# Reordering the opening of a fused retention and MoE kernel: constants, masks, one load and the weight triggers

## The chip, the cores and the metric

The kernel runs on one core of a Trainium2 chip. The metric is the device time of one execution in microseconds. The kernel before the change was run six times: the median is 203.0 us, the lowest 202.28 us, the highest 203.25 us.

A core has five engines that run their own instruction streams in order: TensorE (PE: matrix products and transposes, with weight loads as a row of their own, PEld), VectorE (DVE), ScalarE (ACT), GpSimd (POOL) and SyncE (SP, here only a queue that issues DMAs). They wait for each other by semaphores. ScalarE, GpSimd and SyncE issue DMAs too; each issuing instruction stands in its engine's stream, and whatever follows it there waits for the issue (not for the landing).

## What is computed

```python
# attention: B=4, H=8, S=768, D=64; gamma_h = 1 - 2**(-5-h)
for t in range(S):
    state = gamma * state + outer(k[:, :, t], v[:, :, t])     # D x D per batch and head
    y[:, :, t] = 1/sqrt(D) * q[:, :, t] @ state
x = y.transpose(0, 2, 1, 3).reshape(B * S, H * D)             # 3072 x 512
h = x @ w_in                                                  # 512 -> 2048
g = 0.5 * h * (1 + tanh(sqrt(2/pi) * (h + 0.044715 * h**3)))
out = g @ w_out                                               # 2048 -> 512, 3072 x 512 f32
```

## The kernel before, in words

The sequence of 768 tokens is cut into six chunks of C = 128 tokens. For a chunk c and a batch b the attention is done in matrix form: q and k are scaled by powers of gamma and rounded to fp16 (`prep1`, lines 146 to 164), transposed by TensorE (`mm_T`, line 187) and copied out of PSUM (`ev_T`), multiplied to a 128 x 128 matrix A per head (`mm_A`, line 207), masked with a decay triangle (`ev_A`, line 220, which reads `mask`), and multiplied with v (`mm_yi`, line 242). `ev_Y` writes the result, transposed, to `xT[c]`: that is the input of the first MoE product. `mm_s` and `ev_S` carry the state to the next chunk.

The first MoE product of a chunk has 16 column blocks of w_in; `moe1_two(c, fp, t0, t1)` does blocks 2fp and 2fp+1 for the tokens of two batches (8 matmuls of 128x256, line 349) and one Gelu on ScalarE (line 369). `moe1_four` does four blocks for one batch. w_in comes in four tiles of four blocks each: `w_in0` serves fp 0 and 1, `w_in1` fp 2 and 3, `w_in2` fp 4 and 5, `w_in3` fp 6 and 7. The second product uses sums of g (`g_sums`, line 399) and of w_out (`w_sums`), a product scheme with seven block products in place of eight (`units_0` for chunk 0, `units_w` for the others).

The order on every engine is the order of the calls in the source (`manual_schedule`). This case is about the opening, chunk 0, in these places:

- Lines 96 to 104: loads at the start. On SyncE's queue: k of batch 0, the identity `iden`, k of batch 1, v of batch 1, k of batch 2. On ScalarE's queue: q of batch 0, the constants `cst` (74 KB: the row scales for q and k, the triangle), q of batch 1, v of batch 0; and from line 723 q of batch 2.
- `spin(n)` (line 113): n matmuls of zeros with zeros into a PSUM bank that nobody reads. They keep TensorE busy.
- `masks()` (line 126): eight instructions on VectorE, each scales the triangle in `cst` by a constant of one head. `ev_A` of batch 0 needs all eight.
- `prep1(VE, "q", 0, b)` (VectorE) and `prep1(PO, "k", 0, b)` (GpSimd): the scaled q and k of chunk 0. Both read `cst`.
- `load_w_in(i)` and `load_w_out(i)` (lines 328 and 336): 512 KB each as it lands in fp16, issued by GpSimd between its `prep1` calls. GpSimd also loads v of batch 2 and all of batch 3.
- Lines 740 to 796: the attention of chunk 0, batch by batch, with `spin` calls between, then the first MoE product of chunk 0 with the attention of batches 2 and 3 laid between its parts. `t01` is the tokens of batches 0 and 1, `t2` those of batch 2, `t3` those of batch 3.

After the opening, lines 798 to 1042 run the remaining second and first products and the attention of the later chunks; the change doesn't touch them.

Of the kernel before, what the change touches and what calls it, by code (L numbers as in the profile page):

```python
# [16 lines left out]
def kernel(  # L17
# [9 lines left out]
    nc = tc.nc  # L27
# [21 lines left out]
    cst_h = nc.inline_tensor(cst_np, name="rr_cst")  # L49
# [16 lines left out]
    OQ, OK, OG, OT = 0, H, 2 * H, 2 * H + NHP  # L66


    misc = const.tile([128, 32], F32)
    cst = const.tile([128, 192], F32)  # L70
# [8 lines left out]
    def ld_tile(nm, c, b):  # L79
        if (nm, c, b) not in raw:  # L80
            tag, n = ("v1" if nm == "v" else "qk1", 5 if nm == "v" else 8) if c == 1 else (f"{nm}32", 4)
            raw[nm, c, b] = ld.tile([128, H, Dh], F32, tag=tag, bufs=n, name=f"{nm}32")
        return raw[nm, c, b]

    def load1(eng, nm, c, b):
        eng.dma_start(
            out=ld_tile(nm, c, b),
            in_=srcs[nm][b, :, c * C:(c + 1) * C, :].rearrange("h p d -> p h d"),
        )

    def load(c):
        for b in range(B):
            for nm in "qkv":
                load1(nc.sync, nm, c, b)

    load1(nc.sync, "k", 0, 0)
    load1(nc.scalar, "q", 0, 0)
    nc.scalar.dma_start(out=cst[:, :OT + 128], in_=cst_h.ap())
    nc.sync.dma_start(out=iden, in_=iden_h.ap())
    load1(nc.scalar, "q", 0, 1)  # L100
    load1(nc.sync, "k", 0, 1)
    load1(nc.scalar, "v", 0, 0)
    load1(nc.sync, "v", 0, 1)
    load1(nc.sync, "k", 0, 2)


    zero = const.tile([128, 512], F16, name="zero")
# [2 lines left out]
        out=misc[:, 0:1], in_=zero[:, 0:1], func=AF.Gelu_apprx_tanh, scale=1.0  # L110
    )

    def spin(n):
        ps = bank("h", shape=(128, 512), name="spin_ps")
        for _ in range(n):
            nc.tensor.matmul(
                out=ps, lhsT=zero[:, 0:128], rhs=zero, start=True, stop=True
            )
# [7 lines left out]
    def masks():  # L126
        for j in range(2):
            for hp in range(NHP):
                nc.vector.tensor_scalar(  # L129
                    out=mask[:, j, hp],  # L130
                    in0=cst[:, OT:OT + 128],
                    scalar1=float(1.0 / g128[2 * hp + j]),
                    scalar2=None,
                    op0=ALU.mult,
                )

    h16 = {}
    qk16 = {}

    def copy_on(eng, out, in_):  # L140
        if eng is nc.scalar:
            eng.copy(out=out, in_=in_)  # L142
        else:
            eng.tensor_copy(out=out, in_=in_)

    def prep1(eng, nm, c, b):
        if nm == "v":
            t = pre.tile([128, H, Dh], F16, tag="v16", bufs=6, name="v16")
        else:
            if (c, b) not in qk16:  # L150
                qk16[c, b] = pre.tile([128, 2, H, Dh], F16, tag="qk16", bufs=6, name="qk16")
            t = qk16[c, b][:, "qk".index(nm)]
        src = ld_tile(nm, c, b)
        if (nm == "v") == (c < 1):
            copy_on(eng, t, src)
        else:
            col = OQ if nm == "q" else OK
            eng.tensor_tensor(  # L158
                out=t,
                in0=src,  # L160
                in1=cst[:, col:col + H].unsqueeze(2).broadcast_to([128, H, Dh]),
                op=ALU.mult,
            )
        h16[nm, c, b] = t
# [11 lines left out]
    def bank(tag, dt=F32, shape=(128, NHP, 128), name="ps"):  # L176
        return psum.tile(list(shape), dt, tag=tag, bufs=BANKS[tag], name=name)
# [38 lines left out]
    def ev_A(c, b):  # L216
        ps = pss.pop(("A", c, b))
        for j in range(2):
            s = att.tile([128, NHP, 128], F16, tag=f"a{j}", bufs=2, name=f"a_sb{j}")
            nc.vector.tensor_tensor(out=s, in0=ps[j], in1=mask[:, j], op=ALU.mult)  # L220
            a_sb[c, b, j] = s
# [29 lines left out]
    def ev_Y(c, b, eng=nc.vector):  # L251
        if c not in xT:
            xT[c] = xp.tile([128, NHP, B * C], F16, tag="x", bufs=2, name="xT")
        x, ps = xT[c][:, :, b * C:(b + 1) * C], pss.pop(("Y", c, b))
        if c < 1:
            copy_on(eng, x, ps)
        else:
            nc.vector.tensor_tensor(out=x, in0=ps, in1=dec, op=ALU.mult)  # L258
# [15 lines left out]
    def ev_S(c, bs, engs=(nc.vector, nc.vector)):  # L274
        if c + 1 >= NCk:
            return
        s_ps = pss.pop(("S", c, bs))
        for j in range(2):
            sl = slice(j * 64, (j + 1) * 64)
            t = st[sl, bs[0]:bs[-1] + 1, :, j]  # L280
            if c == 0:
                copy_on(engs[j], t, s_ps[sl])
                continue
            for hp in range(NHP):
                nc.vector.scalar_tensor_tensor(  # L285
                    out=t[:, :, hp],
                    in0=t[:, :, hp],
                    scalar=cst[sl, OG + hp:OG + hp + 1],
                    in1=s_ps[sl, :, hp],
                    op0=ALU.mult,  # L290
                    op1=ALU.add,
                )
# [35 lines left out]
    def load_w_in(i):  # L328
        nc.gpsimd.dma_start(
            out=w_in_sb[i],  # L330
            in_=moe_w_in.rearrange("(kc p) n -> p kc n", p=128)[
                :, :, w_in_at[i] * 128:(w_in_at[i] + w_in_n[i]) * 128
            ],
        )
# [11 lines left out]
    def moe1_mm(c, fc, out, t0, t1):  # L346
        wi, wr = w_in_of[fc]
        for kc in range(NHP):
            nc.tensor.matmul(  # L349
                out=out,  # L350
                lhsT=w_in_sb[wi][:, kc, wr * 128:(wr + 1) * 128],
                rhs=xT[c][:, kc, t0:t1],
                start=(kc == 0),
                stop=(kc == NHP - 1),
                skip_group_check=True,
            )

    def g_tile(c, fc):
        r = fc % 8 // 2 * 2
        return g_sb[fc // 8][:, r:r + 2]  # L360

    def g_q(c, r, b, i):
        if (r, b) == (1, 1) and c > 2 and c % 2:
            return g_odd[:, 4 * i:4 * i + 4]
        g = g_sb[i].rearrange("p (f r) (a b t) -> p r b f a t", r=2, a=2, b=2)
        return g[:, r, b]

    def gelu(out, in_):
        nc.scalar.activation(out=out, in_=in_, func=AF.Gelu_apprx_tanh, scale=1.0)  # L369
# [6 lines left out]
    def moe1_two(c, fp, t0, t1):  # L376

        h_ps = bank("h", shape=(128, 2, B * C // 2), name="h_ps")
        for r in range(2):
            moe1_mm(c, 2 * fp + r, h_ps[:, r, 0:t1 - t0], t0, t1)  # L380
        gelu(g_tile(c, 2 * fp)[:, :, t0:t1], h_ps[:, :, 0:t1 - t0])
# [16 lines left out]
    def tt(eng, out, in0, in1, op):  # L398
        eng.tensor_tensor(out=out, in0=in0, in1=in1, op=op)  # L399
# [8 lines left out]
    def g_sums(eng, c, f0, f1, p0=0, p1=2, keys=(1, 2, 3, 4)):  # L408
        i = f0 % 4
        q = {  # L410
            (r, b): g_q(c, r, b, f0 // 4)[:, i:i + f1 - f0, p0:p1]
            for r in range(2)
            for b in range(2)
        }
        t = {j: s_g[j][:, f0:f1, p0:p1] for j in s_g}
        ops = (
            (1, q[0, 1], q[1, 1], ALU.add),
            (2, t[1], q[0, 0], ALU.subtract),
            (3, q[0, 0], q[0, 1], ALU.subtract),
            (4, q[1, 0], t[2], ALU.subtract),  # L420
        )
        for j, in0, in1, o in ops:
            if j in keys:
                tt(eng, t[j], in0, in1, o)
# [284 lines left out]
    def loads(eng, c, *what):  # L709
        for nm, b in what:  # L710
            load1(eng, nm, c, int(b))
# [7 lines left out]
    VE, AC, PO, SY = nc.vector, nc.scalar, nc.gpsimd, nc.sync  # L719
# [1 line left out]


    load1(AC, "q", 0, 2)
    spin(8)
    prep1(VE, "q", 0, 0)
    masks()
    prep1(PO, "k", 0, 0)
    load_w_in(0)
    prep1(PO, "k", 0, 1)
    loads(PO, 0, "v2")  # L730
    load_w_in(1)
    loads(PO, 0, "k3", "q3", "v3")
    load_w_in(2)
    prep1(PO, "k", 0, 2)
    load_w_in(3)
    prep1(PO, "k", 0, 3)
    for i in range(NO):
# [5 lines left out]
    spin(3)  # L743
    mm_A(0, 0)
    ev_A(0, 0)
    spin(2)
    mm_T(0, 1)
    ev_T(0, 1, AC)
    prep1(AC, "v", 0, 0)
    spin(3)  # L750
    mm_A(0, 1)
    ev_A(0, 1)
    mm_yc(0, 0, "o")
# [1 line left out]
    prep1(AC, "v", 0, 1)  # L755
    ev_Y(0, 0, AC)
    prep1(VE, "q", 0, 2)
    spin(3)
    mm_yc(0, 1, "o")
    mm_yi(0, 1)  # L760
    mm_s(0, (0, 1), "o")
    ev_Y(0, 1, AC)

    t01, t2, t3, t23 = (0, half), (half, half + C), (half + C, 2 * half), (half, 2 * half)
    moe1_two(0, 0, *t01)
# [14 lines left out]
    mm_T(0, 3)  # L780
    ev_T(0, 3)
    prep1(AC, "v", 0, 3)
    g_sums(VE, 0, 0, 4, 0, 1, (1, 2))
    moe1_four(0, 1, *t2)
    moe1_two(0, 4, *t01)
    mm_A(0, 3)
    ev_A(0, 3)
    g_sums(VE, 0, 0, 4, 0, 1, (3, 4))
    moe1_two(0, 5, *t01)
    moe1_two(0, 6, *t01)  # L790
    mm_yc(0, 3, "o")
    mm_yi(0, 3)
    mm_s(0, (2, 3))
    ev_Y(0, 3)
    ev_S(0, (2, 3))
    moe1_two(0, 7, *t01)

    nc.gpsimd.tensor_copy(out=dec[0:1, 0, 0:1], in_=w_out_sb[3][0:1, 0, 0:1])
# [274 lines left out]
```

## Time and profile before

| what | value |
|---|---|
| median of six runs | 203.0 us |
| the profiled execution, its own time | 202.28 us |
| its span, first to last instruction | 200.4 us |
| time of that execution outside the span | 1.9 us |
| PE busy | 192.4 us, 96% of the span |
| DVE, ACT, POOL busy | 138.4, 117.7, 137.6 us |
| granted TensorE clock | 1.000 |
| first matmul of the MoE product starts | 15.21 us into the span |

Two things help to read it. The profile page's second part cuts the span into 40 slices of 5 us and gives the busy tenths: PE is at 7 in the first three slices and at 9 in all the others but the last. And the granted clock is 1.00 in every row, yet the zero matmuls of the first 8 us start about 0.43 us apart and those after 11 us about 0.22 us apart, so a half-speed start of TensorE is seen in the durations and not in that column.

### The profile page before, as it was taken

Reading aid. Unit: us, or ns where it says so; the run is one execution under the profiler, and the core shown is the slowest. Engines: PE = TensorE matmul, PEld = TensorE weight load, DVE = VectorE, ACT = ScalarE, POOL = GpSimd, SP = SyncE. Lnnn points to the kernel's source line nnn. Section 1 sums busy time; section 2 is a strip of 40 time slices with the busy share of each in tenths; the row PEclk is TensorE's granted clock in tenths of the full one; section 3 lists DMA queues with packets and bytes.
Section 4 is the critical chain, followed back from the end, with each engine's and each line's share of the span. In section 5 each row is a group of like instructions: output and inputs, shape, how many; then the busy total and the mean of one; then the engine's idle time right before and its main releaser. Section 6 shows DMA issues by size and latency. Waiting matters only on the chain.

```text
span 200.4 us, 5117 instructions
## 1 busy us (share of the span) xinstructions
PE 192.4 (96%) x2067; PEld 153.4 (77%) x2067; DVE 138.4 (69%) x279; ACT 117.7 (59%) x214; POOL 137.6 (69%) x139
## 2 busy tenths in 40 slices
PE   7779999999999999999999999999999999999993
PEld 2347898877888888745478887888888888888883
DVE  0976699969792449997997975995925945227720
ACT  2266654473589409266657698379494496777321
POOL 3995933945189998769947929389979299598200
PEclk9999999999999999999999999999999999999999
DMA  6999999999996699999989989941400130002205
GB/s 153 287 231 273 206 207 263 343 326 211 328 218 137 153 205 257 184 294 249 208 174 228 214 193 226 101 155 66 105 3 0 77 136 0 0 3 106 108 3 206
DMA packets 83255, 34.25 MB, mean 171 GB/s; under 512 B 75936, under 2 KB 80416, under 8 KB 83232
## 3 DMA queue, kind: packets, MB, share of 16 engines
q1 hardware_dynamic: 71696, 18.65, 44.0%
q0 software_dynamic: 6944, 13.63, 25.5%
q10 hardware_dynamic: 4592, 1.65, 3.1%
q8 instruction: 16, 0.26, 0.6%
q14 instruction: 7, 0.06, 0.1%
HBM read 27.63 MB, written 6.29 MB: 169 GB/s over the span
## 4 chain that ended last, share of the span: by engine, by line
PE 89%; DVE 5%; DMA 2%; ACT 2%; issue 1%; ACTq 0%; DVEq 0%
PE o_ps L510 31%; PE h_ps L349 20%; PE h_ps L592 19%; PE y_ps L242 4%; PE a_ps L207 3%; PE o_ps L630 3%; PE o_ps L663 3%; PE y_ps L229 2%; DMA cst<-rr_cst 2%; DVE mask L129 2%; PE qkT_ps L187 2%; DVE a_sb L220 1%; PE s_ps L266 1%; DVE qk L158 1%; DVE xT L258 1%
## 5 line engine op out<-in xcount | busy, mean ns | idle before, releaser
L349 PE MATMUL h_ps<-xT,w_in 128*128 128x256 f16 (+2 forms) x352 | 45.9, 282 | 0.4 <-ACT xT L142 0.4
L369 ACT ACTIVATE g<-h_ps 128x512 f16<-128x512 f32 x52 | 31.0, 600 | 19.7 <-PE h_ps L349 18.0
L399 POOL TENSOR_TENSOR s_g<-g 128x512 f16<-128x512 f16 x30 | 35.3, 1183 | 7.5 <-ACT g L369 6.5
L220 DVE TENSOR_TENSOR a_sb<-a_ps,mask 128x512 f16<-128x512 f32 x48 | 30.5, 683 | 13.3 <-PE a_ps L207 11.9
L349 PEld LDWEIGHTS <-w_in 128*128 128x128 f16 x352 | 30.4, 98 | 10.8 <-issue 0.6
L510 PEld LDWEIGHTS <-s_g 128*128 128x128 f16 x320 | 30.7, 98 | 4.2 <-POOL s_g L399 0.3
L369 ACT ACTIVATE g<-h_sb 128x512 f16<-128x512 f32 x36 | 21.9, 632 | 17.5 <-DVE h_sb L399 17.3
L399 DVE TENSOR_TENSOR h_sb<-h_ps,h_sb 128x512 f32<-128x512 f32 x36 | 22.9, 684 | 9.6 <-ACT h_sb L142 8.9
L510 PE MATMUL o_ps<-t_w,s_g 128*128 128x256 f16 x240 | 29.4, 273 | 0.0
L158 POOL TENSOR_TENSOR v<-v,cst 128x512 f16<-128x512 f32 x20 | 20.5, 1046 | 7.5 <-DMA v<-in_v_dram 3.8
L510 PEld LDWEIGHTS <-g 128*128 128x128 f16 x208 | 20.2, 98 | 2.5
L399 POOL TENSOR_TENSOR s_g<-s_g,g 128x512 f16<-128x512 f16 x18 | 20.9, 1162 | 1.4
L399 POOL TENSOR_TENSOR s_g<-g,s_g 128x512 f16<-128x512 f16 x18 | 20.6, 1154 | 0.0
L592 PEld LDWEIGHTS <-t_in 128*128 128x128 f16 x192 | 18.0, 98 | 2.9
L142 ACT COPY h_sb<-h_ps 128x512 f32<-128x512 f32 x36 | 19.1, 598 | 1.3 <-PE h_ps L592 1.3
L510 PE MATMUL o_ps<-w_out,g 128*128 128x256 f16 x160 | 19.1, 273 | 0.0
L285 DVE SCALAR_TENSOR_TENSOR st<-st,cst,s_ps 64x128 f16<-64x128 f16 x64 | 18.2, 346 | 0.2
L592 PE MATMUL h_ps<-s_x,t_in 128*128 128x256 f16 x144 | 17.8, 273 | 0.0
L258 DVE TENSOR_TENSOR xT<-y_ps,dec 128x512 f16<-128x512 f32 x20 | 13.3, 684 | 5.4 <-PE y_ps L242 5.3
L592 PEld LDWEIGHTS <-w_in 128*128 128x128 f16 x144 | 14.1, 98 | 1.8
L142 ACT CAST qk<-q 128x512 f16<-128x512 f32 x20 | 12.6, 631 | 2.2 <-DMA q<-in_q_dram 2.2
L142 ACT CAST qk<-k 128x512 f16<-128x512 f32 x20 | 12.6, 630 | 0.1
(81 smaller groups left out, 274.8 us busy)
## 6 DMA issues: line engine op xcount, KB each, us to landing
out_dram<-o_sb POOLq DMA_DIRECT2D x10, 512.0 KB, 3.2
k<-in_k_dram SPq DMA_DIRECT2D x19, 256.0 KB, 4.8
v<-in_v_dram SPq DMA_DIRECT2D x17, 256.0 KB, 4.6
q<-in_q_dram SPq DMA_DIRECT2D x16, 256.0 KB, 5.0
w_in<-in_moe_w_in_dram POOLq DMA_DIRECT2D x4, 512.0 KB, 8.3
w_out<-in_moe_w_out_dram POOLq DMA_DIRECT2D x4, 512.0 KB, 10.7
v<-in_v_dram POOLq DMA_DIRECT2D x6, 256.0 KB, 7.0
k<-in_k_dram POOLq DMA_DIRECT2D x5, 256.0 KB, 7.6
```

What stands on the lines that cost most here:

```text
L142: eng.copy(out=out, in_=in_)
L158: eng.tensor_tensor(out=t, in0=src, in1=cst[:, col:col + H].unsqueeze(2).broadcast_to([128, H, Dh]), op=ALU.mult,)
L207: nc.tensor.matmul(out=ps[j][:, hp], lhsT=t[j * 64:(j + 1) * 64, 1, hp], rhs=t[j * 64:(j + 1) * 64, 0, hp], start=True, stop=True,)
L220: nc.vector.tensor_tensor(out=s, in0=ps[j], in1=mask[:, j], op=ALU.mult)
L242: nc.tensor.matmul(out=y_ps[j * 64:(j + 1) * 64, hp], lhsT=h16["v", c, b][:, 2 * hp + j], rhs=a_sb[c, b, j][:, hp], start=(c == 0), stop=True,
L258: nc.vector.tensor_tensor(out=x, in0=ps, in1=dec, op=ALU.mult)
L285: nc.vector.scalar_tensor_tensor(out=t[:, :, hp], in0=t[:, :, hp], scalar=cst[sl, OG + hp:OG + hp + 1], in1=s_ps[sl, :, hp], op0=ALU.mult, ...
L349: nc.tensor.matmul(out=out, lhsT=w_in_sb[wi][:, kc, wr * 128:(wr + 1) * 128], rhs=xT[c][:, kc, t0:t1], start=(kc == 0), stop=(kc == NHP - ...
L369: nc.scalar.activation(out=out, in_=in_, func=AF.Gelu_apprx_tanh, scale=1.0)
L399: eng.tensor_tensor(out=out, in0=in0, in1=in1, op=op)
L510: nc.tensor.matmul(out=po, lhsT=lhs(c, lk, fp, a), rhs=rhs(rk, fp), start=(new and fp == 0 and (last or a == 0)), stop=(stop and fp == NP ...
L592: nc.tensor.matmul(out=self.ps[G, k][:, p], lhsT=self.lhs(lk, 2 * G + p, kc), rhs=self.rhs(rk, kc), start=(new and p == 0 and kc == 0), st ...
```

## The change

Five things are done, all in the opening. (1) `cst` is the first DMA on ScalarE's queue, ahead of q of batch 0. (2) `masks()` stands ahead of `prep1` of q of batch 0 on VectorE. (3) v of batch 2 is loaded by SyncE's queue, behind k of batch 2, and no more by GpSimd. (4) GpSimd copies one element of the scaled q of batch 0 to a scratch tile before it issues `load_w_in(0)`; so it waits there until VectorE has written that q. k of batch 2 is scaled on VectorE and no more on GpSimd. (5) The counts of the `spin` calls change (8 to 10, 2 to 0, 3 to 4, and 2 new ones ahead of the MoE product), and two parts of the MoE product and the g sums are called in another order.

```diff
+    nc.scalar.dma_start(out=cst[:, :OT + 128], in_=cst_h.ap())
     load1(nc.sync, "k", 0, 0)
     load1(nc.scalar, "q", 0, 0)
-    nc.scalar.dma_start(out=cst[:, :OT + 128], in_=cst_h.ap())
     nc.sync.dma_start(out=iden, in_=iden_h.ap())
...
     load1(nc.sync, "k", 0, 2)
+    load1(nc.sync, "v", 0, 2)
...
     load1(AC, "q", 0, 2)
-    spin(8)
+    spin(10)
+    masks()
     prep1(VE, "q", 0, 0)
-    masks()
     prep1(PO, "k", 0, 0)
+    nc.gpsimd.tensor_copy(out=misc[0:1, 2:3], in_=h16["q", 0, 0][0:1, 0, 0:1])
     load_w_in(0)
     prep1(PO, "k", 0, 1)
-    loads(PO, 0, "v2")
     load_w_in(1)
     loads(PO, 0, "k3", "q3", "v3")
     load_w_in(2)
-    prep1(PO, "k", 0, 2)
     load_w_in(3)
     prep1(PO, "k", 0, 3)
...
     ev_A(0, 0)
-    spin(2)
     mm_T(0, 1)
     ev_T(0, 1, AC)
     prep1(AC, "v", 0, 0)
-    spin(3)
+    spin(4)
     mm_A(0, 1)
...
     prep1(VE, "q", 0, 2)
+    prep1(VE, "k", 0, 2)
     spin(3)
...
     ev_Y(0, 1, AC)
+    spin(2)
...
-    g_sums(VE, 0, 0, 4, 0, 1, (1, 2))
     moe1_four(0, 1, *t2)
-    moe1_two(0, 4, *t01)
     mm_A(0, 3)
     ev_A(0, 3)
-    g_sums(VE, 0, 0, 4, 0, 1, (3, 4))
+    g_sums(VE, 0, 0, 4, 0, 1)
+    moe1_two(0, 4, *t01)
     moe1_two(0, 5, *t01)
-    moe1_two(0, 6, *t01)
     mm_yc(0, 3, "o")
...
     ev_S(0, (2, 3))
+    moe1_two(0, 6, *t01)
     moe1_two(0, 7, *t01)
```

## The prediction

> **What bounds the kernel now.** I read the busy slices first: PE stands at 9 tenths from slice 4 to the end, so after about 15 us time can only be won by starting that full stretch sooner or by waiting less inside it. Next the chain of waits from 0 to 20 us (start, duration, what):
>
> ```profile
> 1.26 3.98 DMA cst<-rr_cst
> ...
> 5.34 0.69 DVE qk L158
> 6.03 3.96 DVE mask L129 x8
> 10.00 0.61 DVE qk L158
> ...
> 10.65 0.64 PE qkT_ps L187 x8
> ...
> 11.31 1.01 ACT qkT L142
> 12.32 0.53 ACT v L142
> ...
> 14.57 0.59 ACT xT L142
> ...
> 15.21 1.03 PE h_ps L349 x8
> ```
>
> The constants come at 5.24, q of batch 0 is scaled, and then eight mask instructions hold VectorE for 4 us; q of batch 1 waits behind them, and with it that batch's transposes, masked product, y, xT and the first MoE matmul at 15.21. The group of the masks tells why they take so long (minimum, median, maximum in ns):
>
> ```profile
> L129 DVE TENSOR_SCALAR mask<-cst x8: 206/390/1903, 6.0 to 9.8; 128x128 f32<-128x128 f32 x8
> ```
>
> One alone takes 0.21 us; the long ones (1.07 and 1.90) begin while GpSimd works on k of batch 0 (5.39 to 6.94), issues w_in0 (6.88 to 7.81) and works on k of batch 1 (7.83 to 8.88). Two engines hinder each other.
>
> The second bound is the DMA. Its share is over 1 from 2.5 us to past 35 us. Which queue moved in 7.5 to 9.5, and which in 10.5 to 12.5 (packets, MB, share):
>
> ```profile
> q10 hardware_dynamic: 1232, 0.31, 68.8%
> q1 hardware_dynamic: 1054, 0.27, 58.8%
> ```
> ```profile
> q0 software_dynamic: 406, 0.43, 124.3%
> ```
>
> w_in0 was issued at 6.88 on GpSimd's queue (q0), yet moved nothing until SyncE's and ScalarE's queues were empty, at about 9.9. Issue to landing of w_in0 (issued 6.88) and w_in1 (9.77):
>
> ```profile
> w_in<-in_moe_w_in_dram POOLq DMA_DIRECT2D x1, 512.0 KB, 6.3
> ```
> ```profile
> w_in<-in_moe_w_in_dram POOLq DMA_DIRECT2D x1, 512.0 KB, 7.6
> ```
>
> So w_in0 lands at 13.2, w_in1 at 17.4, and by the same sum w_in2 at 22.2 (13.15 + 9.0), w_in3 at 24.6 (14.92 + 9.7), k of the next chunk's batch 0 at 36.4 (23.07 + 13.3). First uses: 15.21, 17.82, about 22.9, about 25.0, 37.85. TensorE waits for none, but w_in1 has 0.4 us to spare and w_in3 0.4.
>
> **The change part by part.**
>
> *Constants first, masks first.* In the row above, `cst` landed last of the first three transfers on two queues, at 5.24, q of batch 0 at 4.85 and k at 4.4. All three together are the same bytes, so with `cst` first, q lands at about 5.2 and `cst` some 0.25 us of moving (74 KB at 288 GB/s) after the first packets at 2.5: about 3.3 with the same tail. From 3.3 VectorE has the masks alone: 8 x 0.21 = 1.7, until 5.0. GpSimd gets k at about 4.4; either it takes its 1.05 us between two masks, or it starts at 5.0 and then holds up q's scaling. Both ways masks, k and q of batch 0 are all done near 5.0 + 1.05 + 0.69 = 6.7. Were there no hindering: 5.9. If GpSimd stretches the masks as before: 3.3 + 4.05 + 0.69 = 8.0. I take 6.7. Transposes of batch 0 then run in one piece, 0.62 to 1.0, and end at 7.3 to 7.7, against 7.6 before: nothing won here.
>
> *What follows.* `ev_T` 1.01 to about 8.5, `mm_A` to 9.0; its masking starts at 9.0 in place of 10.52, since the masks are there. GpSimd: copy of one element (the like copy to `dec` takes 0.40) at 6.7, w_in0's issue 0.93 to 8.0, k of batch 1 1.05 to 9.1. q of batch 1 (lands 7.3) is scaled by 8.1. So batch 1's transposes start at about 9.2, against 10.65; the same steps as before in the chain, 15.17 - 10.65 = 4.5, give xT of batch 1 at about 13.7. Chain alone: 1.4 us won.
>
> *v of batch 2 to SyncE's queue.* It is 256 KB ahead of w_in0: 0.91 us at 288 GB/s. In GpSimd's queue it went at 379 GB/s (row of 12.5 to 13.0), 0.69 us. **A rule against the trace:** the Trainium skill, "DMA: Bandwidth & Descriptors", section on queues, rings and completion order, says that each DMA engine goes round between the queues with work, a packet at a time. By that, w_in0 would get its share from about 8 and the move would cost it little: it lands near 13.2 and the MoE starts with the chain at 13.7, 1.4 won. By the rows above a later queue waits for what was issued earlier: w_in0 lands at 13.2 + 0.9 = 14.1, and the MoE starts then, 1.0 won. I take the row. What comes behind, w_in1 and later, moves by 0.91 - 0.69 = +0.2. On SyncE only the load of `dec` (36.8 before) stands behind it: nothing. On ScalarE the issue of `cst` (0.73) now precedes that of q (0.50): q, q of batch 1 and v of batch 0 are issued up to 0.2 later, and the saturated engines hide it.
>
> *w_in's triggers behind q.* Hidden: w_in0 is issued by 8.0 and its turn comes at 10.8. The cover ends if the issue slips past 10. Queued behind the copy on GpSimd are w_in0, k of batch 1, w_in1, three loads of batch 3, w_in2 and w_in3; all are issued by about 14, ahead of their turns.
>
> *k of batch 2 on VectorE.* 0.69 at about 13, after q of batch 2 (landed 10.7); VectorE was idle from 15.58 to 16.73 and its next task is the transposes' copy at about 15.7. Nothing. GpSimd loses 1.09 at 13.93; nothing hung on it, k of batch 3 waited for its load.
>
> *Spins.* Two net more by count: 2 more ahead of the first transposes (1.19 + 10 x 0.43 = 5.5, TensorE has no work before 6.7), 2 ahead of the MoE (0.43, while w_in0 is on its way). Nothing, if w_in0 is the gate; 0.3 if xT is.
>
> *Order of the MoE parts.* The same matmuls. fp 4 comes 0.3 later and fp 6 0.8 later (y and the state of batch 3 go ahead of it): this gives w_in2 and w_in3 time. On VectorE four sums (0.35 us apart in the rows at 29.8 to 31.3) stand ahead of xT of batch 3: done near 25.7, needed at 26.3. Nothing.
>
> *Sum.* Opening -1.0. At w_in1: needed at 17.82 - 1.0 = 16.8, landing by the row 17.4 + 0.2 = 17.6, a loss of 0.8; but that landing tells of a last straggling engine: v of batch 2 moved by 13.0 (the rate is 379 GB/s before and 219, w_in's, after) but landed at 14.6 (8.82 + 5.8), and w_in1's own rate ends at 15.5, where 348 GB/s begin, yet it landed at 17.4. The straggle begins in a load that is no longer ahead of w_in1. Without the straggler 16.6. I take a loss of 0.2, bounds 0 and 0.8. At the next chunk's first transposes: cast of k ends 36.99 + 0.2 = 37.2, needed 36.85: 0 to 0.35, I take 0. Later chunks: 0. **In all -0.8** (bounds -1.4 and -0.1 for this case): the execution of 202.28 becomes 201.5. It was the fastest of the six, 0.7 below the median; against the median of 203.0 that is **202.2 us**.
>
> **The rivals.**
>
> *The loads give the gain back* (22%). The straggler stays, w_in1 gates fp 2 at 17.6 and k of chunk 1 the transposes at 37.2. For: transfers saturated until past 35 us, so their ends don't move with TensorE. Against: the spare times at w_in2 and w_in3 grow. Gain 0.1 to 0.5: 202.7.
>
> *The change doesn't clear VectorE* (8%). Masks and GpSimd hinder each other from 4.4 on, q is scaled at 8.0; 1.3 later than in my sum uses up the 1.4 of the chain. For: the 1903 ns. Against: GpSimd has one instruction there in place of three. 203.0, give or take 0.3.
>
> *TensorE stays at half speed* (15%), the slower case. The zero matmuls show it: 3 in 1.49 us at 7.39, 3 in 0.81 at 11.11. The Trainium skill, "TensorE: Matmul & The Clock Gate", section on what is actually happening, gives full speed after one busy window of about 3.4 us, the windows running freely. The trace had 3.60 us of zero matmuls from 1.19 and was still slow at 7.39, so an aligned window counts: by the rule 8 spins fill one with a chance of (3.6 - 3.4)/3.4, some 6%, 10 spins with (4.3 - 3.4)/3.4, some 26% (estimates). So I expect the switch about where it was, near 9. But two spins at 9.35 are gone and batch 1's transposes come sooner; if the window that closes there counts as idle, the next is 3.4 later. It decides from the first MoE matmul: at half speed eight of 128x256 take 1.7 in place of 0.87, and transposes and A of batch 1 0.2 to 0.4 more each. One window later costs about 1 and eats the gain; two windows cost 3.4 x 0.5 = 1.7 more in full matmuls: +0.7 to +1.7 net, 204.2. Against: no gap above 1.3 us in TensorE's row, and more spins ahead.
>
> **How the numbers follow.** My case has 55%: 202.2, own range 201.6 to 202.8. Some 0.3%, 0.6 us, is what a measurement can tell from no change. The loads have 22%, VectorE 8%, the clock 15%. Faster by more than that: 49 of my 55 and 6 of the loads' 22, 0.55. Within: 5 of mine, 15 of the loads', 8 of VectorE's, 2 of the clock's, 0.30. Slower: 13 of the clock's, 1 each of mine and of the loads' (a late weight that I don't see), 0.15. Range 201.4 to 203.7: low end a win of 1.6, upper end the mild half of the clock case.
>
> **What would show each step.** In the new profile: `cst` from issue to landing under 3 us and masks of median near 0.21, done by 5.5; scaled q of batch 0 ending near 6.7; batch 1's transposes near 9.2; the first MoE matmul at 14.1 to 14.3 with w_in0 (not xT) as what it waited for; fp 2 near 16.8 to 17.6; the chunk-1 transposes near 37. Wrong if w_in0 moves before v of batch 2 ends, if zero matmuls after 11 us are 0.43 apart, or if a row of waits on w_in1 exceeds 0.8.

## The result: no measurable change, 1.0013 of the time before

| | before | after |
|---|---|---|
| median of the shared runs, us | 202.95 (72 runs) | 203.85 (35 runs) |
| ratio after / before, 95% interval | | 1.0013 [0.9993, 1.0033] |
| profiled execution, its own time / span, us | 202.28 / 200.4 | 203.31 / 201.5 |
| PE / DVE / POOL busy, us | 192.4 / 138.4 / 137.6 | 192.8 / 136.4 / 135.7 |
| first matmul of the MoE product, us | 15.21 | 14.69 |
| second product of chunk 0 starts, us | 32.61 | 32.62 |
| last matmul starts, us | 197.12 | 197.79 |

Thirteen executions of the kernel after (206.4 to 207.7 us, at a granted clock of 0.98 to 0.99) lift its median and are left out of the ratio. By the ratio the time is 203.2 us, where 202.2 was forecast.

The chain of waits in the opening did get shorter, far more than the result shows. The masks of after (the group by tile; minimum, median, maximum in ns):

```profile
L130 DVE TENSOR_SCALAR mask<-cst x8: 220/223/227, 3.3 to 4.3; 128x128 f32<-128x128 f32 x8
```

All eight now take the short time; they end at 4.48, before q of batch 0 has landed. The chain of waits of after, 0 to 16 us (start, duration, what):

```profile
1.15 4.23 DMA q<-in_q_dram
...
5.40 0.70 DVE qk L159
...
6.16 0.12 POOL misc L729
6.28 8.37 DMA w_in<-in_moe_w_in_dram
...
14.69 1.05 PE h_ps L350 x8
```

The masks are gone from the chain, and so are the transposes, `ev_T`, v and xT. Batch 1's transposes start at 8.36 (10.65 before) and its xT is done at 13.06 (15.16): 2.1 us won. But one piece has taken the place of all of them: w_in0, 8.37 us from issue to landing, where before it took 6.3. TensorE's part of the timeline (start, duration, what; in brackets the idle time ahead of it and what ended it) shows the wait:

```profile
14.69 1.05 PE L350 MATMUL h_ps<-xT,w_in 128*128 128x256 f16 x8 [1.46 <-DMA w_in<-in_moe_w_in_dram]
...
23.03 1.92 PE L350 MATMUL h_ps<-xT,w_in 128*128 128x256 f16 x16 [0.34 <-ACT g L370]
...
25.58 1.38 PE L350 MATMUL h_ps<-xT,w_in 128*128 128x256 f16 x11
```

So 0.52 of the 2.1 is left at the first MoE matmul. The rest of it goes at the next tiles. Adding the time to landing to the time of issue: w_in1 lands at 8.68 + 8.7 = 17.38, w_in2 at 12.12 + 10.9 = 23.02, w_in3 at 12.87 + 12.7 = 25.57; their first users start at 17.39, 23.03 and 25.58. The second of these is named `ACT g` in the row, since a Gelu ended within 0.03 us of the landing, and at 25.58 another Gelu ends with w_in3; TensorE's weight loads show the transfer:

```profile
PEld L350 <- DMA w_in<-in_moe_w_in_dram: 2.6, 3, 2.0
```

Three waits, 2.6 us, the longest 2.0 (from the waits of 0 to 30 us). Which of the two, Gelu or transfer, holds the later matmuls is settled by e1 and e4 below. Before, TensorE waited for no tile of w_in; after, it starts on each of the four in the moment it lands. From 26.5 us to 93.6 the matmuls of both kernels stand at the same times to 0.02 us.

What held up w_in0 is in the queues (q0 is GpSimd's, q1 SyncE's, q10 ScalarE's). v of batch 2 was issued by SyncE at 6.16, w_in0 by GpSimd at 6.28. Both from issue to landing, then what the queues moved in 12.0 to 12.5 us (packets, MB, and the time of the packets as a share of 16 engines' time; the two shares add up to more than 100%, so packets overlap on an engine):

```profile
w_in<-in_moe_w_in_dram POOLq DMA_DIRECT2D x1, 512.0 KB, 8.4
v<-in_v_dram SPq DMA_DIRECT2D x1, 256.0 KB, 9.4
```
```profile
q0 software_dynamic: 75, 0.08, 90.0%
q1 hardware_dynamic: 77, 0.02, 29.8%
```

The packets alternate, 75 to 77: a 1 KB packet of w_in0, a 256-byte packet of v. It goes so from about 11 to 14 us. Before, w_in0 had the engines to itself there (the row of 10.5 to 12.5 shown above), and v of batch 2 followed it in the same queue.

One more loss lies far from the change. VectorE in 88 to 93 us, before, then after:

```profile
88.23 1.38 DVE L399 TENSOR_TENSOR t_in<-w_in 128x512 f16<-128x512 f16 x1
89.53 1.37 DVE L399 TENSOR_TENSOR t_in<-w_in,t_in 128x512 f16<-128x512 f16 x1
90.82 2.47 DVE L220 TENSOR_TENSOR a_sb<-a_ps,mask 128x512 f16<-128x512 f32 x4
```
```profile
88.08 1.35 DVE L400 TENSOR_TENSOR t_in<-t_in,w_in 128x512 f16<-128x512 f16 x1
89.35 1.37 DVE L400 TENSOR_TENSOR t_in<-w_in 128x512 f16<-128x512 f16 x1
90.64 1.37 DVE L400 TENSOR_TENSOR t_in<-w_in,t_in 128x512 f16<-128x512 f16 x1
91.94 2.47 DVE L221 TENSOR_TENSOR a_sb<-a_ps,mask 128x512 f16<-128x512 f32 x4
```

Such a sum takes 0.42 us, but 1.37 while GpSimd makes its sums of g (`s_g`, from 88.0 in both kernels). VectorE is 0.2 later in after, and so a third sum falls into that stretch. The masking of A starts 1.12 later, TensorE waits 0.39 us for it at 94.46 (`a_ps` on `a_sb`), and its matmuls stand 0.71 later from 94.8 on and 0.67 later at the last one. That is 0.67 of the 1.1 us between the two profiled spans; the rest comes behind the last matmul.

### The profile page after: what moved, and what is told of

Read it like the earlier page. It is cut to its first block, busy times and chain, and to the rows that moved or that the text cites. A ratio compares the mean times of both kernels' runs of the same rounds, so it can differ in the third digit from the quotient of the medians.

```text
span 201.5 us, 5123 instructions
## 1 busy us (share of the span) xinstructions
PE 192.8 (96%) x2070; PEld 153.5 (76%) x2070; DVE 136.4 (68%) x280; ACT 117.7 (58%) x214; POOL 135.7 (67%) x138
## 4 chain that ended last, share of the span: by engine, by line
PE 87%; DMA 6%; DVE 3%; ACT 1%; issue 1%; ACTq 0%; POOL 0%; DVEq 0%
PE o_ps L511 31%; PE h_ps L350 20%; PE h_ps L593 19%; DMA w_in<-in_moe_w_in_dram 4%; PE y_ps L243 3%; PE o_ps L631 3%; PE a_ps L208 3%; PE o_ps L664 3%; DMA q<-in_q_dram 2%; PE y_ps L230 2%; DVE a_sb L221 2%; PE qkT_ps L188 1%; PE s_ps L267 1%; ACT g L370 1%; DVE xT L259 1%
## 5 line engine op out<-in xcount | busy, mean ns | idle before, releaser
L370 ACT ACTIVATE g<-h_ps 128x512 f16<-128x512 f32 x52 | 31.0, 600 | 22.6 <-PE h_ps L350 20.9
L221 DVE TENSOR_TENSOR a_sb<-a_ps,mask 128x512 f16<-128x512 f32 x48 | 30.5, 684 | 13.5 <-PE a_ps L208 12.4
L593 PE MATMUL h_ps<-s_x,t_in 128*128 128x256 f16 x144 | 17.8, 273 | 0.0
L593 PEld LDWEIGHTS <-w_in 128*128 128x128 f16 x144 | 14.1, 98 | 1.8
L400 POOL TENSOR_TENSOR s_g<-g,g_odd 128x512 f16<-128x512 f16 x6 | 6.9, 1156 | 9.0 <-ACT h_sb L143 9.0
```

What stands on the lines that cost most here:

```text
L593: nc.tensor.matmul(out=self.ps[G, k][:, p], lhsT=self.lhs(lk, 2 * G + p, kc), rhs=self.rhs(rk, kc), start=(new and p == 0 and kc == 0), st ...
```

## The experiments

Each kernel was profiled and timed against the kernel before; ratios have 95% intervals. L in the expectations is the theory that the loads of w_in took the gain, M the theory that the new order of the MoE parts did. Where matmuls start in the profiled executions (us):

| | first MoE | first on w_in2 | second product | chunk 1's transposes | last |
|---|---|---|---|---|---|
| before | 15.21 | 22.70 | 32.61 | 37.85 | 197.12 |
| after | 14.69 | 23.03 | 32.62 | 37.86 | 197.79 |
| e1 | 13.26 | 22.60 | 32.18 | 37.42 | 196.62 |
| e3 | 13.44 | 22.19 | 32.47 | 37.71 | 196.91 |
| e4 | 13.17 | 21.60 | 31.16 | 36.40 | 195.67 |
| e5 | 14.56 | 22.60 | 32.19 | 37.43 | 196.63 |
| e7 | 13.36 | 21.85 | 31.43 | 36.67 | 195.94 |
| e9 | 14.77 | 22.71 | 32.29 | 37.53 | 196.82 |
| e10 | 13.93 | 23.59 | 33.50 | 38.74 | 197.95 |
| e11 | 14.19 | 23.38 | 32.96 | 38.20 | 197.40 |

(e2, e6, e8 and e12 are told below. The third column is the first matmul that reads w_in2; before, e3 and e10 have the old order of parts.)

### e1: v of batch 2 back on GpSimd's queue, the rest as after

```diff
     load1(nc.sync, "k", 0, 2)
-    load1(nc.sync, "v", 0, 2)
...
     prep1(PO, "k", 0, 1)
+    loads(PO, 0, "v2")
     load_w_in(1)
```

> The changed kernel with one part undone: v of batch 2 is loaded by GpSimd ahead of w_in1, as before. Theory L (the loads gate TensorE: w_in0, w_in2, w_in3, then k of chunk 1): w_in0 lands near 13.3 in place of 14.65, the first MoE matmul starts there, w_in2 and w_in3 come 0.5 to 1 sooner, the second product starts near 31.9 in place of 32.62, the transposes of chunk 1 near 37.1 in place of 37.86; in time about 0.7 under the changed kernel, near 202.4. Theory M (the new order of the MoE parts costs, since fp 4 and the part at 25.6 wait for a Gelu of ScalarE): the first MoE matmul is sooner too, but the two waits ahead of fp 4 and ahead of fp 6 stay, 0.3 each or more, whenever w_in2 and w_in3 land; the second product not before 32.3.

Measured: **0.9908 [0.9882, 0.9935]**, median 201.74 us: faster than both kernels. TensorE's timeline shows waits for three tiles:

```profile
13.26 1.05 PE L349 MATMUL h_ps<-xT,w_in 128*128 128x256 f16 x8 [0.30 <-DMA w_in<-in_moe_w_in_dram]
...
16.50 1.05 PE L349 MATMUL h_ps<-xT,w_in 128*128 128x256 f16 x8 [0.55 <-DMA w_in<-in_moe_w_in_dram]
...
22.60 1.92 PE L349 MATMUL h_ps<-xT,w_in 128*128 128x256 f16 x16 [0.57 <-DMA w_in<-in_moe_w_in_dram]
```

w_in0 lands at 13.2, as before the change, and in 10.5 to 12.5 GpSimd's queue alone moves (407 packets, 125.6%). The MoE starts 1.43 sooner than in after. Still each tile gates: of 1.95 won against before at the first matmul, 0.43 is left at the second product. So moving v of batch 2 cost 1.4 at the start and 0.4 by 32 us in these executions. Theory M had the second product not before 32.3; it starts at 32.18.

The ratio is better than these traces say: their spans are 200.4 (before), 199.9 (e1), 201.5 (after), 0.2% between before and e1. TensorE's granted clock makes part of the difference. In this round before ran 29 of 53 times at 0.983 (mean 204.2 us) and 23 times at 0.997 or more (mean 202.9), e1 14 of 16 times at 0.997 or more (mean 201.9) and never at 0.983. At equal clock e1 is 0.5% faster than before, not 0.9%. What a clock of 0.983 is, the trace of e2 shows.

### e2: v of batch 2 on SyncE's queue, alone

```diff
     load1(nc.sync, "k", 0, 2)
+    load1(nc.sync, "v", 0, 2)
...
-    loads(PO, 0, "v2")
     load_w_in(1)
```

> The kernel before with one part of the change alone: v of batch 2 on SyncE's queue. Theory L: w_in0 lands near 14.6, still under 15.21, so the first MoE matmul stays at 15.2; w_in2 lands near 23.0 and w_in3 near 25.6 in place of 22.2 and 24.6, fp 4 (22.9) waits 0.1, fp 6 (25.0) waits 0.6; second product 0.6 later, 33.2; time +0.6, near 203.5. Theory M: this order has no such waits, second product at 32.6, time as before.

Measured: 0.9996 [0.9964, 1.0027]; the expected loss did not come. Here v's issue (5.15 to 6.75) was over when that of w_in0 began (6.76), and the queues did not alternate. What they moved in 10.5 to 11.0 us, and w_in0 from its issue to its landing:

```profile
q1 hardware_dynamic: 506, 0.13, 112.7%
q0 software_dynamic: 16, 0.02, 19.4%
```
```profile
w_in<-in_moe_w_in_dram POOLq DMA_DIRECT2D x1, 512.0 KB, 7.3
```

In 11.0 to 11.5 it was 37 and 97 packets. So w_in0 landed at 6.76 + 7.3 = 14.1 and w_in1 at 8.70 + 7.9 = 16.6: with v going first and alone, both land where the prediction had put them (14.1, and 16.6 without a straggler). The loss of 0.9 at w_in0 does not show in the time because xT, behind the old masks, comes later still: at 16.1 in this execution, and at 15.2 in the profiled one of before. The move alone does nothing where the chain hides it.

This execution ran at a granted clock of 0.983. The page's row of the clock in 40 slices of 5 us, and two places of TensorE's timeline:

```profile
PEclk9859999999999999999999999999999999999999
```
```profile
7.11 0.81 PE L117 MATMUL spin_ps<-zero 128*128 128x512 f16 x3
...
11.22 1.49 PE L117 MATMUL spin_ps<-zero 128*128 128x512 f16 x3
```

TensorE was at full speed at 7.11 already (three zero matmuls in 0.81 us), earlier than in the profiled execution of before, then fell back to half (three in 1.49, granted clock 0.50 from 10 to 14 us) until about 15. In the trace of e6, whose opening is that of before, it went the same way, and the first MoE matmul came at 16.39 in place of 15.21. The fallback does show in the clock column, unlike the slow start.

So the kernel before comes in two kinds of executions: in the three later rounds 105 at a clock of 0.997 or more (means of 202.4 to 202.9 us by round) and 85 at 0.983 (203.7 to 204.2). The profiled one is of the first kind. With the masks first alone (e3) none of 22 ran at 0.983, and of the kernel after one of 36: an effect of the change that neither the prediction nor the chain of waits has in it. Against before at 0.997 or more, the kernel after at the same clock (22 executions, mean 203.2) is 0.2% to 0.4% slower: an estimate, since the rounds differ. No run was made to show why TensorE falls back in some executions, or that the executions at 0.983 without a trace are all of this kind; half speed for some 7 of 202 us gives that mean.

### e3: constants first and masks first, alone

```diff
+    nc.scalar.dma_start(out=cst[:, :OT + 128], in_=cst_h.ap())
     load1(nc.sync, "k", 0, 0)
     load1(nc.scalar, "q", 0, 0)
-    nc.scalar.dma_start(out=cst[:, :OT + 128], in_=cst_h.ap())
...
-    prep1(VE, "q", 0, 0)
     masks()
+    prep1(VE, "q", 0, 0)
     prep1(PO, "k", 0, 0)
```

> The kernel before with the constants first and the masks first, nothing else. Theory L: VectorE is free by 5, xT of batch 1 is there by about 13.3, w_in0 as before at 13.2, so the first MoE matmul starts near 13.5 to 14; but w_in1 (17.4 before, if its last engine straggles again) holds fp 2, w_in2 (22.2) fp 4 and w_in3 (24.6) fp 6, so that the second product starts near 32.2 and the gain in time is about 0.4. Theory M (loads do not matter): the whole 1.5 gained at the first MoE matmul stays, second product near 31.1, time near 201.5.

Measured: 0.9978 [0.9954, 1.0002], and TensorE's waits in 12 to 36 us:

```profile
PE h_ps L349 <- DMA w_in<-in_moe_w_in_dram: 1.8, 3, 1.1
PE h_ps L349 <- ACT g L369: 0.7, 1, 0.7
```

The two moves make the whole shortening of the chain (first MoE matmul at 13.44, already waiting 1.06 for w_in0), and w_in takes back nearly all of it by 32 us, 0.14 being left. At a granted clock of 0.997 or more its mean is 202.8, that of before in the same round 202.9: what is left of the ratio is the fewer executions at 0.983. Here w_in3 is the last gate: the chain of waits runs through k of batch 2 on GpSimd (0.97), behind which w_in3 is issued at 14.41. In e1, with that scaling on VectorE, w_in3 is issued at 13.5.

### e4: v of batch 2 not loaded

```diff
-    load1(nc.sync, "v", 0, 2)
+    raw["v", 0, 2] = raw["v", 0, 1]
```

This leaves out one load of 256 KB; batch 2 uses the v of batch 1.

> The changed kernel without the load of v of batch 2 in chunk 0 (batch 1's v is used in its place): 256 KB less to move, no instruction less for TensorE, VectorE or ScalarE. Theory L: w_in0 near 13.2, and all later weights about 0.9 to 1 sooner than in the changed kernel; first MoE matmul near 13.3, second product near 31.6, transposes of chunk 1 near 36.9; time 0.9 under the changed kernel, near 202.2. Theory M: waits ahead of fp 4 and fp 6 stay, second product not before 32.3, gain at most 0.3.

Measured: **0.9858 [0.9813, 0.9903]**. First MoE matmul at 13.17, with 0.4 us of waiting for w_in left in 12 to 36 us, and the second product 1.46 sooner than in after. The order of the MoE parts is that of after, and theory M, which had the second product not before 32.3, falls: it starts at 31.16. The transfers are what the opening ends on: 256 KB less gives over 1 us. At a granted clock of 0.997 or more the time is 1.0% under before (six executions, mean 200.8).

### e5, e6, e7: GpSimd's sums of chunk 2 one part later (on after, on before, on e1)

```diff
-            3: [(g_sums, PO, 2, 0, 2)],
-            4: [(att_AY, 3, (), "att", 3, (0, 1), None)],
+            4: [(att_AY, 3, (), "att", 3, (0, 1), None), (g_sums, PO, 2, 0, 2)],
```

> The changed kernel; GpSimd's first g sums of chunk 2 are called one MoE part later, behind the attention call there. In the profile of the changed kernel three of VectorE's twelve w_in sums at 84 to 92 us run 1.36 in place of 0.42 us beside GpSimd's sums, and TensorE loses 0.67 at 93.7; before the change two are stretched and nothing is lost. Theory O (this collision far behind the opening, not the opening, makes the changed kernel's typical execution slower than the best of before): none or one stretched sum, no wait at 93.7, the same times up to there, the time 0.7 or more under the changed kernel, near 202.6. Rival P (the collision is one profile's accident and the time is made in the opening alone): the time as the changed kernel's, 203.2 to 203.6.

> The kernel before with the same shift of GpSimd's first g sums of chunk 2. Theory O: its executions spread from 202.1 to over 204 since two or three sums are stretched by chance; with the shift they gather near 202.3, 0.3 to 0.5% under the median of before. Rival P: no difference.

> The changed kernel with v of batch 2 back on GpSimd's queue and the same shift of the g sums. Theory L and O together: near 201.5, since the kernel with v of batch 2 alone put back had one stretched sum and few slow executions; 0 to 0.3 under it. Rival P: as that kernel, 201.7.

Measured: e5 0.9997 [0.9961, 1.0033], e6 0.9979 [0.9952, 1.0007], e7 0.9924 [0.9893, 0.9955]. In the trace of e5 one sum takes 1.38 in place of three, nothing waits at 94, and the span is 200.4 against 201.5; e7 has two long sums and no wait either. So a shift of GpSimd's sums takes the wait away. (The trace of e6 is one at a clock of 0.983, with the first MoE matmul at 16.39, and isn't compared.) In time none of the three is told from its parent by the intervals, so how often the collision costs something stays open. e5 and e7 show one thing more: their openings are the same code as those of after and e1, and yet w_in2 was there at 22.6 in place of 23.0, and by 21.85 in place of 22.6. Landings differ by 0.4 to 0.8 us between executions: w_in0, too, landed at 14.65 in after, at 14.5 in e5 and at 13.9 in e10, which have the same opening up to there. Differences of that size between two single traces aren't the effect of an edit.

### e8: e1 without the copy that delays w_in0's issue

```diff
     prep1(PO, "k", 0, 0)
-    nc.gpsimd.tensor_copy(out=misc[0:1, 2:3], in_=h16["q", 0, 0][0:1, 0, 0:1])
     load_w_in(0)
```

> The changed kernel with v of batch 2 back on GpSimd's queue and without GpSimd's copy that waits for the scaled q of batch 0, so w_in0 is issued near 5.2 in place of 5.84. Theory L with queues that serve what was issued earlier: w_in0's turn still comes when SyncE's and ScalarE's queues run dry, it lands near 13.1, the time stays within 0.3 of that kernel. Rival R (w_in0 goes round with the other queues as soon as its descriptors are written): w_in0 moves from about 7.5 on and delays v of batch 0, k and q of batch 2; batch 0's v is cast later than 9.9 and the first MoE matmul moves to 13.6 or later, or w_in0 lands by 12.5 and the first MoE matmul starts near 12.9.

Measured: 0.9939 [0.9913, 0.9964], not told from e1. The trace shows what comes without the copy: w_in0 is issued at 4.95, while SyncE is still at the issue of k of batch 2 (3.17 to 5.66). It now alternates with k of batch 2 (10.5 to 11.0: 78 and 74 packets), and batch 2's transposes are late: the part behind them starts at 15.29 in place of 14.59. At w_in1 most of it is gone (16.65 against 16.50), since that tile gates there anyway. So the sharing of rival R came, but little of its delay: the first MoE matmul starts at 13.44. The sharing is no property of v of batch 2: it came here with another load of SyncE's queue whose issue overlaps that of w_in0.

### e9: after, w_in0 issued behind k of batch 1

```diff
-    load_w_in(0)
     prep1(PO, "k", 0, 1)
+    load_w_in(0)
     load_w_in(1)
```

> The changed kernel with GpSimd's issue of w_in0 moved behind its scaling of k of batch 1, to about 8.5, well after SyncE has issued v of batch 2 (6.16). Theory S (the loss at w_in0 is a sharing of the engines: v of batch 2 and w_in0 were issued at the same time, 6.16 and 6.28, and went packet by packet until 14): v of batch 2 now goes alone, its queue is dry by 11 and w_in0 lands near 14.0 in place of 14.65; the first MoE matmul near 14.1; the rate of GpSimd's queue is full from 11 on. In time 0.2 to 0.5 under the changed kernel. Rival F (each queue has its turn by issue; v of batch 2 just stands ahead): w_in0 at 14.65 as before or later, since it is issued later.

Measured: 0.9978 [0.9959, 0.9997]. The queues in 10.5 to 11.0, and in 12.0 to 12.5:

```profile
q1 hardware_dynamic: 402, 0.10, 89.0%
q0 software_dynamic: 14, 0.01, 46.8%
```
```profile
q0 software_dynamic: 97, 0.10, 121.6%
```

The sharing is gone: v goes alone and lands sooner (5.9 us from issue in place of 9.4), then w_in0 goes alone. But w_in0 itself lands at 8.85 + 5.88 = 14.73, no sooner than in after (14.0 was expected, and rival F had 14.65 or later): SyncE's queue fills the engines to about 11.0, and then 11.0 to 11.5 is filled to 71% only. The later tiles come sooner (the matmuls on w_in2 at 22.71). So ending the sharing by a later issue wins nothing at w_in0; how much of the 1.5 us is v and how much the issue, 2.6 us later than in after, this run can't tell.

### e10: after with the old order of the MoE parts

```diff
+    g_sums(VE, 0, 0, 4, 0, 1, (1, 2))
     moe1_four(0, 1, *t2)
+    moe1_two(0, 4, *t01)
     mm_A(0, 3)
...
-    moe1_two(0, 6, *t01)
     moe1_two(0, 7, *t01)
```

> The changed kernel with the calls from fp 4 on in the order of before (fp 4 ahead of A of batch 3, fp 6 ahead of y of batch 3, the g sums in two halves). Theory L (w_in2 and w_in3 gate fp 4 and fp 6): A and y of batch 3 no longer fill the waits, the second product starts near 33.1 in place of 32.62; time 0.3 to 0.6 over the changed kernel. Theory M (the new order itself costs the 0.3 waits): the second product near 32.3 or sooner, time 0.3 under the changed kernel.

Measured: 1.0049 [1.0026, 1.0071], 0.4% over after, where the two intervals only just meet. So the old order wins nothing back. That the new order helps isn't shown: the second product starts at 33.50, but in this execution v of batch 2 landed late, `y` of batch 2 waited for it, and the chain of waits runs from there.

```profile
5.98 12.77 DMA v<-in_v_dram
18.75 0.02 issue
18.77 0.62 ACT v L143
```

(the chain of waits: 12.8 us from issue to landing in place of 9.4. Here w_in0 got more of the engines and landed at 13.9, and v paid for it. The prediction had no cost for a late v.)

### e11: e7 with k and q of batch 2 on GpSimd too, w_in0 behind k of batch 1

```diff
-    load1(nc.sync, "k", 0, 2)
...
-    load1(AC, "q", 0, 2)
...
-    nc.gpsimd.tensor_copy(out=misc[0:1, 2:3], in_=h16["q", 0, 0][0:1, 0, 0:1])
-    load_w_in(0)
+    loads(PO, 0, "k2", "q2")
     prep1(PO, "k", 0, 1)
+    load_w_in(0)
     loads(PO, 0, "v2")
```

> The changed kernel with v of batch 2 back on GpSimd and the g sums of chunk 2 later (the fastest so far), and with k and q of batch 2 loaded by GpSimd too, ahead of w_in0, whose issue stands behind the scaling of k of batch 1; no copy to wait for. Theory L (the train of loads sets the time; 256 KB takes 0.91 us on SyncE's and ScalarE's queues and 0.69 on GpSimd's): all weights 0.4 sooner, w_in0 near 12.8, w_in3 near 23.8; v of batch 0 later by up to 1.4 as the queues share; time 0.2 to 0.4 under that kernel, near 201.2. Rival: the sharing delays k and q of batch 1 or v of batch 0 by more than the train gains, first MoE matmul past 14.2, time as that kernel or 0.3 over it.

Measured: 1.0017 [0.9997, 1.0036], the rival's side, and slower against e7 (0.9924) than the rival had it. The higher rate of GpSimd's queue is not had for nothing: from 9.5 to 11 us the queue moves at shares of 29% to 48%, while its loads are issued one by one, and q of batch 3 (issued 11.99, landed 20.41) is late and its transposes with it.

### e12: after with the old counts of zero matmuls

```diff
-    spin(10)
+    spin(8)
...
+    spin(2)
     mm_T(0, 1)
...
-    spin(4)
+    spin(3)
...
-    spin(2)
```

> The changed kernel with the zero matmuls counted as before (8, 2, 3, none ahead of the MoE product). If the counts matter only for when TensorE goes to full speed: transposes of batch 0 and the zero matmuls behind them at half speed (3 in 1.49 us), masked product of batch 1 some 0.5 to 1 later, xT of batch 1 near 13.8 at the latest, still ahead of w_in0 at 14.65; first MoE matmul at 14.7, time unchanged within 0.3. Otherwise, if TensorE stays at half speed up to the MoE product: first MoE matmuls of 1.7 us, time 1 over the changed kernel.

Measured: 1.0025 [0.9996, 1.0054]. TensorE, at two places of its timeline:

```profile
7.13 1.49 PE L117 MATMUL spin_ps<-zero 128*128 128x512 f16 x3
...
15.12 1.03 PE L350 MATMUL h_ps<-xT,w_in 128*128 128x256 f16 x8 [0.42 <-ACT xT L143]
```

Three zero matmuls in 1.49 us: half speed, to about 12 us. The chain is then the gate, and the MoE starts at 15.12 (14.7 or less was expected). The second product starts at 32.53 all the same, 17.41 us behind the first MoE matmul, as before (17.40): starting later, TensorE finds every tile of w_in there, where after loses 0.5 us to them (17.93). In after the three took 0.81 at 6.77. The counts go with that, but don't decide it alone: in all nine profiled executions with 10 zero matmuls at the start (after, e1, e4, e5, e7 to e11) the three behind batch 0's transposes take 0.81 to 0.85; of the five with 8, they take 1.49 in before and e12 and 0.81 in e2, e3 and e6, and of these only e3 stays at full speed.

## Where the prediction held and where it failed, step by step

The 203.2 us lie inside the range of 201.4 to 203.7, and "no change" had 0.30. But the main case (55%, 202.2, own range 201.6 to 202.8) did not come. What came is the rival of the loads at 22%, and it too was put 0.5 too low. The range held because it was wide enough for the rivals. There was luck in it as well: the measured ratio contains executions of before at a granted clock of 0.983 (shown at e2), which the prediction did not know of and which, by the estimate there, hide a loss of 0.2% to 0.4%.

- **Constants and masks first.** Right, and undersized. 1.4 us of chain were forecast, 2.1 came. `cst` took 2.5 us to land, as hoped. The scaled q was done at 6.09 and not 6.7: the masks took 1.18 in all, not 1.7, and ended at 4.48, before q of batch 0 landed and 0.17 after GpSimd began on k. Some more came from TensorE at full speed from about 6.5 us on: the three zero matmuls behind batch 0's transposes took 0.81 in place of 1.49.
- **w_in's triggers behind q.** Hidden, as said. The copy holds w_in0's issue to 6.28, sooner than the 7.0 or so that was forecast, and e8 gave it no price.
- **v of batch 2 to SyncE's queue. This step failed, by the size of its term and by the overlap that it left out.** It was priced at 0.91 us for w_in0 ("w_in0 lands at 13.2 + 0.9 = 14.1") and at "0.91 - 0.69 = +0.2" for all that follows. Measured: w_in0 at 14.65, +1.45; w_in1 at 17.38, near the row's 17.6 and not at the 16.6 that I hoped for without a straggler; w_in2 +0.8 and w_in3 +1.0 (in e5, with the same opening, +0.35 and +0.5). 0.91 was a load that has the engines to itself at 288 GB/s. Where that was so, in e2, the forecast came true (14.1 and 16.6). In after it was not so: a packet of 256 B took 17.8 ns of an engine when alone (after, 6.0 to 6.5: 518 packets, 115.4% of 16 engines in 0.5 us), and 31.0 ns when they alternate with packets of 1 KB (77, 29.8%). With some 500 of them from 11 to 14.5 us, that is 500 x 13.2 ns / 16 = 0.4 us more, an estimate that gives most of the missing 0.5. In 10 to 15 us the engines moved 207 GB/s against 230 before, 0.11 MB less, half a microsecond of w_in's rate. The size is not a fixed one: with the same opening, w_in0 lost 1.3 in e5 and 0.7 in e10, where v came last.
- **Rule against row.** I took the row, and each was half the truth. Which goes first was as the row said: w_in0 moved nothing until about 10, while loads that were issued before it stood in the other queues. From there the counts agree with what the Trainium skill says ("DMA: Bandwidth & Descriptors", the section on queues, rings and completion order), queue by queue, a packet at a time: 75 to 77. In before, e1 and e2 they didn't share so. My conclusion from that rule, a w_in0 near 13.2, was wrong as well, since half the packets of ten to fourteen went to v. That w_in0 "moves before v of batch 2 ends" had been named as a sign against my case.
- **Spare time at w_in2 and w_in3.** I let the new order give them time (0.3 and 0.8) and stopped at w_in1. But a gain at the start makes every later use sooner, while transfers that are saturated stay: TensorE was ready for w_in2 at 22.69 (A of batch 3, 22.29 + 0.40), and it came at 23.02. At w_in1, priced at 0.2, 0.07 was lost (the step from A of batch 2 took 0.40 in place of 0.33), at w_in2 0.34, at w_in3 the last 0.1 (0.45 in place of 0.35).
- **Later chunks: 0.** Wrong in the profiled execution, by 0.67 us from 94 on: the collision of VectorE's and GpSimd's sums. How often it comes is open.
- **k of chunk 1.** Forecast at 37.2, its cast ended at 37.86, when the transposes start: no slack, and no loss of its own.
- **The rivals.** "The loads give the gain back" is what happened, put at 22%; it named w_in1 and k of chunk 1 where w_in0, w_in2 and w_in3 did it. "The change doesn't clear VectorE" fell (masks at 0.22 each). "TensorE stays at half speed" did not happen in the profiled execution of after; e12 shows that a half-speed start costs the first MoE matmul 0.4 but not the second product. Whether it happened in others isn't shown. The chances that I worked out from the Trainium skill ("TensorE: Matmul & The Clock Gate", the section on what is actually happening) for full speed at an early time were far too low by these runs: 26% for 10 zero matmuls, where it came in nine of nine, and 6% for 8, where it came in three of five.

## What to carry to other kernels

Where transfers are saturated, a shorter chain moves the wait to the next tile, and the one after: compare the landing of **every** tile with its new use, not of the first alone. Put nothing ahead of the tile that will be waited for, in whatever queue: here the same 256 KB cost 0.7 to 1.45 us ahead of w_in0, and behind it in w_in0's own queue the same change is faster than before, by 0.9% in all and 0.5% at equal granted clock (e1). And read the granted clock of each execution before two kernels are compared by their times.

## What the hardware showed beside this

- Where two queues shared the engines (after, e5, e8, e10, e12), they alternated packet by packet although the packets differ in size, so 256-byte packets beside 1 KB packets got a fifth of the bytes (0.02 of 0.10 MB), and each took 31 ns of an engine where it took 18 among packets of its own size.
- Whether they alternate went, in these runs, by the overlap of the two issuing instructions: v 6.16 to 7.19 and w_in0 from 6.28 (after), k of batch 2 3.17 to 5.66 and w_in0 from 4.95 (e8) alternate; v to 6.75 and w_in0 from 6.76 (e2), v to 7.55 and w_in0 from 8.85 (e9) do not. e5, e10 and e12, with issues that overlap, alternate too; e3 (3.23 to 5.79 and from 5.10) does so only weakly (24 to 96 packets in 10.5 to 11.0). That is a pattern of a few cases; no run was made for it alone.
- In e11 w_in0 was issued at 8.67 on GpSimd's queue, and from 9.5 no other queue moved anything; still the engines were filled to 29% to 48% until 11.0 and to 129% from 11.5. Why isn't known.
- In these traces VectorE's fp16 sums (128x512) take 0.42 us alone and 1.37 beside GpSimd's sums; its masks (128x128, f32) 0.22 alone and up to 1.90 beside GpSimd's scaling and issue.
- TensorE reached full speed by about 7 us in nine of nine profiled executions with 10 zero matmuls (3.8 to 4.5 us of them) at the start and stayed there, and in three of five with 8 (3.6 us); two of these three (e2, e6) fell back to half speed, granted clock 0.50, from about 8.4 to 15 us.
